# Last stage of a fused attention and state-space backward kernel: another order of its loads, shared tiles, and repeated columns copied on the chip

## The chip, the cores and the metric

The kernel runs on one core of a Trainium2 chip. The metric is the device time of one execution in microseconds (us). Lower is better. Every time below is from the timed runs, or from one execution taken by the hardware profiler, whose page and trace are queried in many views. PE is TensorE, PEld its weight loads, DVE VectorE, ACT ScalarE, POOL GpSimd, SP SyncE, which issues most of the transfers here.

## What is computed

The reference is the backward pass (and the output) of a gated mix of two branches over a sequence of 2048 tokens and 576 channels, in bf16:

```
g = sigmoid((x * gate_w).sum(-1))
a = attention(x, wqkv) @ wo                 # 32 heads of 18 channels
b = ssm_convolution(u = constant, A, B, C, log_dt) + skip   # 128 complex states per channel
out = g * a + (1 - g) * b
grads of x, wqkv, wo, A, B, C, log_dt, Dskip, gate_w for a given grad_out
```

In the last stage these are left: the output itself, the gradient of x (out_1), of wqkv (out_2), of wo (out_3), of the six parameter matrices A, B, C (out_4 to out_9, each 576 x 128), and some vectors.

## The kernel before

The kernel has a first stage (projections), an attention stage, a state-space stage in 18 blocks of 32 channels (for i in range(NBLK)), and the last stage, from about line 1563 to line 1778, which alone is changed. Tiles of 128 partitions are used throughout. The work of the last stage, in the order of the code:

**Loads on SP (lines 1589 to 1610).** zz takes four rows of precomputed state powers (par_d), dt_b the time steps, Wri two more rows of par_d, prm5 the six parameter matrices, wo_sb the matrix wo, wqkvT the transposed wqkv in ten transposing transfers, O_tok the attention output of all 16 token tiles (columns 0 to 575 by one transfer, line 1607, and columns 576 to 639, a repetition of the last 64, by another, line 1608), go_all the whole gradient, gate_b a broadcast row. Each transfer waits on SP until the place that it fills is no longer read, and SP issues strictly in its order. Where a tile lies, and so whose readers it must wait for, is decided by the pools (pf, pfx, pfw, pbwork, pbot): a pool opened after others were closed takes their addresses.

**dwq (line 922).** dwq(u, cs) computes one column quarter u of the gradient of wqkv for chunks cs of 128 rows: 16 matmuls of 427 or 448 columns each into one PSUM tile (tag "one", two buffers), an ACT copy to dwq_bf (three buffers), and a store on POOL's queue. Quarter 2 is loaded into a tile of its own late in the last block; quarters 1 and 3 lie in tiles of tag E1n. dwq_last does the last 64 rows of quarters 2 and 3 together.

**Parameter chain on DVE (lines 1634 to 1681).** Some 60 elementwise operations of 128 x 576 turn the sums SS and CK of the state-space stage into the six parameter gradients. It begins with eight operations on the rows Zr, Zi, then the two negations of Wri (lines 1634 and 1635), then four groups of four with zr, zi, then products with Wr, Wi and the parameter matrices. Each finished matrix is multiplied by dt into a padded tile opad (six of them), turned on PE in five 128 x 128 transposes (emit_dn, line 1619: PSUM tile opt, two buffers), copied by ACT (obo, two buffers) and stored by POOL. PE's order of this part is written by hand: dwq(1), dwq(2), the first two opt, two chunks of dwq(3), two opt, the rest of dwq(3), dwq_last, two opt, and two small matmuls fr.

**Token loop (lines 1690 to 1737).** For each of 16 token tiles t: every fourth t the transposed attention output OT4 of four tiles is made by a transposing transfer out of O_tok; every second t the rows y_b and dxr_b of two tiles are loaded from yd_d (which the last block of the state-space stage still writes: the store of line 807); dqT, the transposed gradient of qkv, is made by two transposing transfers. PE computes ps_a = OT4 @ wo (10 matmuls) and ps_dx = J @ dxr + dqT @ wqkvT (30 matmuls), both in the PSUM tag ps2b with two buffers. DVE forms dif = ps_a - y, o0b (the output rows), an accumulation with go_all, and o1b (the x gradient, from ps_dx); POOL stores o0b and o1b. Buffers: y_b and dxr_b four each, dqT three, o0b three, o1b two, dif two, OT4 two.

**Tail.** A row of 64 small matmuls for gate_w (pgw), then the wo gradient (ps_dwo, 160 matmuls over all token tiles) and its stores.

A hand-written order (manual_schedule) holds for PE and SP in the first part; elsewhere the order is found by a scheduler when the program is built. Every transfer of SP uses one of eight completion semaphores in turn, so it also waits for the transfer eight places ahead of it to have landed.

Of the kernel before, what the change touches and what calls it, by code (L numbers as in the profile page):

```python
# [9 lines left out]
A = mybir.AluOpType  # L10
ACT = mybir.ActivationFunctionType
BF = mybir.dt.bfloat16
F32 = mybir.dt.float32
# [4 lines left out]
P = 128  # L18


def build(tc, aps, dbg_aps=None, stages=("s1", "attn", "post", "s4", "final")):
    nc = tc.nc
# [39 lines left out]
    with ExitStack() as gctx:  # L62
# [66 lines left out]
        with ExitStack() as ctx:  # L129
# [183 lines left out]
            def tt(o, a, b, op):  # L313
                V.tensor_tensor(o, a, b, op=op)
# [1247 lines left out]
        if "final" in stages and "s4" in stages:  # L1562
# [7 lines left out]
            with ExitStack() as ctx:  # L1570
# [9 lines left out]
                tt(ggo, g_t, omg_t, A.mult)  # L1580

                with ExitStack() as actx:
                    actx.enter_context(tc.manual_schedule(engines={mybir.EngineType.PE, mybir.EngineType.SP}))
                    pf = actx.enter_context(tc.tile_pool(name="pf", reuse_waits="tile", bufs=1))
                    Q["nob"] = 3
                    pfw = Q["pbw"] = actx.enter_context(tc.tile_pool(name="pfw", reuse_waits="tile", bufs=2))

                    zz = pf.tile([P, 4, D], F32, name="zz")
                    for q, r_ in enumerate((0, 2, 8)):
                        n_ = 2 if r_ == 8 else 1  # L1590
                        nc.sync.dma_start(zz[:, q:q + n_, :], par_d[:, r_:r_ + n_, :])
                    dt_b = pf.tile([P, D], F32, name="dt_b5")
                    nc.sync.dma_start(dt_b, dt_d)
                    prm5 = pf.tile([P, 6, D], BF, name="prm5")
                    pfx = actx.enter_context(tc.tile_pool(name="pfx", reuse_waits="tile", bufs=1))
                    Wri = pfx.tile([P, 2, D], F32, name="Wri_f")
                    nc.sync.dma_start(Wri, par_d[:, 6:8, :])
                    Wr_n, Wi_n = Wri[:, 0, :], Wri[:, 1, :]
                    nc.sync.dma_start(prm5, prm_d)
                    nc.sync.dma_start(wo_sb[:, 0:nf, :], wo[0:nf * P, :].rearrange("(c p) n -> p c n", p=P))  # L1600
                    for x in range(2):
                        nc.sync.dma_start(wo_sb[x * HB:(x + 1) * HB, nf, :], wo[nf * P:D, :])
                    dwq(1, range(nf), "one", 2)
                    for c, (d0, dsz) in enumerate(dch):
                        for k0_, k1_, f0 in ((0, FZ // P, 0), (FZ // P, FC, FZ - ZP)):
                            nc.sync.dma_start_transpose(out=wqkvT[:, k0_:k1_, d0:d0 + dsz], in_=wqkv[d0:d0 + dsz, f0:f0 + (k1_ - k0_) * P])
                    nc.sync.dma_start(O_tok[:, :, 0:D], O_d)
                    nc.sync.dma_start(O_tok[:, :, D:DPAD], O_d[:, :, D - HB:D])
                    nc.sync.dma_start(go_all, go_v)
                    nc.sync.dma_start(gate_b, gate_w.rearrange("(o d) -> o d", o=1).to_broadcast([P, D]))  # L1610
                    dwq(2, range(nf), "one", 2)

                    opad = []
                    for q in range(6):
                        o_q = pf.tile([P, DPAD], BF, name=f"opad{q}")
                        nc.gpsimd.memset(o_q[:, D:DPAD], 0.0)
                        opad.append(o_q)

                    def emit_dn(out_ap, a, b, idx):
                        o_q = opad[idx]  # L1620
# [10 lines left out]
                    Ar_n, Ai_n, Br_n, Bi_n, Cr_n, Ci_n = [prm5[:, r_, :] for r_ in range(6)]  # L1631
                    ta = pf.tile([P, D], F32, name="fta")
                    o_t = pf.tile([P, D], F32, name="o_t")
                    nc.vector.tensor_scalar(Wr_n, Wr_n, -1.0, None, op0=A.mult)
                    nc.vector.tensor_scalar(Wi_n, Wi_n, -1.0, None, op0=A.mult)
                    Zr_, Zi_, zr_, zi_ = [zz[:, q, :] for q in range(4)]
# [7 lines left out]
                    for (Sr_, Si_, u, kc) in ((S0r, S0i, 0, 0), (S1r, S1i, 2, 1)):  # L1644
# [3 lines left out]
                        nc.vector.scalar_tensor_tensor(Si_, ta, -1.0, CK[:, 1, kc, :], op0=A.mult, op1=A.subtract)  # L1648
                    glr, gli, Tdt = zr_, zi_, s_[0]
                    tt(glr, Wr_n, S1r, A.mult); tt(ta, Wi_n, S1i, A.mult); tt(glr, glr, ta, A.add)  # L1650
# [7 lines left out]
                    dwq(3, (0, 1), "one", 2)  # L1658
# [4 lines left out]
                    dwq(3, range(2, nf), "one", 2)  # L1663
# [4 lines left out]
                    Tb = pf.tile([P, D], BF, name="Tb")  # L1668
                    nc.vector.tensor_copy(Tb, Tdt)
                    row = pf.tile([1, D], F32, name="dlrow")  # L1670
# [4 lines left out]
                    rowb = pf.tile([1, D], BF, name="dlrowb")  # L1675
                    nc.vector.tensor_copy(rowb, row)
                    nc.gpsimd.dma_start(aps_out["out_10"].rearrange("(o d) -> o d", o=1), rowb)
                    rowb2 = pf.tile([1, D], BF, name="ddsrowb")
# [3 lines left out]
                work = ctx.enter_context(tc.tile_pool(name="pbwork", reuse_waits="tile", bufs=2))  # L1682
                wot = ctx.enter_context(tc.tile_pool(name="pbot", reuse_waits="tile", bufs=2))
                sgo = pb.tile([P, NT], F32, name="sgo")
                dsg = pb.tile([P, NT], F32, name="dsg")
                dsgb = pb.tile([P, NT], BF, name="dsgb")
                OT4 = None
                YB = 2
                for t in range(NT):
                    if t % TB == 0:  # L1690
                        OT4 = wot.tile([P, TB, DC, P], BF, tag="OT4", name="OT4")
                        nc.sync.dma_start_transpose(out=OT4.rearrange("p t c q -> p (t c) q"),
                                                    in_=O_tok[:, t:t + TB, :].rearrange("p t d -> p (t d)"))
                    if t % YB == 0:
                        y_b = work.tile([P, YB, D], BF, tag="y_b", bufs=4, name="y_b")
# [124 lines left out]
```

## Times and profile before

| | us |
|---|---|
| timed runs: median (lowest, highest of 3) | 2711.42 (2704.62, 2716.91) |
| profiled execution | 2694.2 |
| its span | 2692.3 |
| its mean granted TensorE clock | 0.97 |
| misc matmuls of the last block, start | 2523.0 |
| first ps_a of the token loop, start | 2579.4 |
| last ps_dx of the token loop, end | 2669.1 |
| ps_dwo, start and length | 2670.2, 17.8 |

How to read the views. The busy table gives, for stretches of time, the busy us of each engine with the number of instructions, then the granted TensorE clock as a share of full speed, the mean busy share of the 16 DMA engines (which can exceed 1 where packets overlap), and GB/s. The view of waits says which engine waited for whom, with the total, the number of waits and the longest. The timeline lists instructions with start and length; for a transfer on SP the length is the time that the queue took to issue it, not the time until it landed. The chain of waits goes back from the last instruction, at each step to what released it.

On the page DVE is busy 85%, PE 89% and ACT 87% of the span; in the last 150 us ACT and POOL are mostly idle and the DMA engines are busy 0.9 or more nearly until the token loop ends.

### The profile page before, as it was taken

To read this page: it belongs to the slowest core of one execution; us is meant where nothing else is said; L and a number is where in the kernel's file an instruction comes from. 1 tells how busy PE (TensorE), PEld (TensorE's weight loads), DVE (VectorE), ACT (ScalarE), POOL (GpSimd) and SP (SyncE) were. 2 spreads that over 40 slices of the span, in tenths; PEclk is the share of its full clock that TensorE was granted. 3 is DMA by queue.
4 is the path that set the end of the run, shared out by engine and by line. 5 is a ranking of instruction groups with operands and counts; after the bars stand their busy time and mean duration, and the time that the engine had idled before them with its cause. 6 is when DMAs were issued, how large, how long until landed. Compare 5 with 4: busy or idle time off the path is not lost.

```text
span 2692.3 us, 70041 instructions
## 1 busy us (share of the span) xinstructions
PE 2404.9 (89%) x27411; PEld 1138.0 (42%) x27411; DVE 2300.6 (85%) x4142; ACT 2343.5 (87%) x2726; POOL 1786.8 (66%) x2829
## 2 busy tenths in 40 slices
PE   8898888998989899998989989898987799999889
PEld 4433333333333333333333333333322689998556
DVE  5649899999989999898999999899986599999854
ACT  5489999999999999999999999999984599898211
POOL 0278888888888888888878888887811144445321
PEclk9889999999999999999999999999996799999989
DMA  7637789879978978987998898789769788887895
GB/s 231 187 98 161 153 167 173 168 156 184 171 150 168 185 155 163 181 168 153 167 177 155 160 179 161 154 168 177 147 131 212 184 246 259 252 255 235 233 265 124
DMA packets 1158165, 485.71 MB, mean 180 GB/s; under 512 B 1072581, under 2 KB 1112118, under 8 KB 1155530
## 3 DMA queue, kind: packets, MB, share of 16 engines
q1 hardware_dynamic: 1112074, 341.62, 63.7%
q0 software_dynamic: 43744, 134.11, 18.3%
q10 hardware_dynamic: 2016, 5.51, 0.7%
q8 instruction: 214, 3.51, 0.6%
q14 instruction: 117, 0.96, 0.1%
HBM read 145.94 MB, written 93.21 MB: 89 GB/s over the span
## 4 chain that ended last, share of the span: by engine, by line
ACT 39%; PE 25%; DVE 24%; issue 6%; DMA 3%; POOL 2%; SPq 1%; ACTq 0%; DVEq 0%; POOLq 0%
ACT eb L1384 23%; ACT PT L1379 15%; DVE ds L1389 7%; PE ps_P L30 7%; DVE tz L730 3%; PE accV L30 2%; PE ps_dx L30 2%; PE turn_p L1092 2%; PE ps_proj L30 2%; DVE tz L733 2%; DVE HG L735 1%; DVE wa L749 1%; DVE wb L749 1%; DVE pq L810 1%; PE accK L30 1%
## 5 line engine op out<-in xcount | busy, mean ns | idle before, releaser
L1389 DVE TENSOR_TENSOR ds<-ps_P,PT 128x512 bf16<-128x512 f32 x2048 | 1312.2, 683 | 122.9 <-PE ps_P L30 84.8
L1384 ACT ACTIVATE eb<-ps_P 128x1024 bf16<-128x1024 f32 x1024 | 1101.2, 1076 | 30.6 <-PE ps_P L30 30.5
L1379 ACT ACTIVATE PT<-ps_P 128x1024 bf16<-128x1024 f32 x1024 | 1106.3, 1081 | 19.6 <-PE ps_P L30 18.4
L30 PE MATMUL ps_P<-dOaT,VaT_g 32*128 32x512 bf16 x2048 | 580.6, 387 | 31.3 <-DVE ds L1389 15.8
L503 POOL TENSOR_TENSOR et<-eG,eT 128x448 f32<-128x448 f32 x576 | 542.2, 961 | 10.7
L30 PE MATMUL ps_P<-QaT_g,KaT_g 32*128 32x512 bf16 x2048 | 400.8, 384 | 137.8 <-ACT PT L1379 124.4
L30 PE MATMUL ps_P<-KaT_g,QaT_g 32*128 32x512 bf16 x2048 | 404.9, 388 | 2.1 <-ACT eb L1384 1.6
L30 PEld LDWEIGHTS <-KaT_g 32*128 32x128 bf16 x2048 | 147.9, 91 | 467.6 <-issue 451.3
L503 POOL TENSOR_TENSOR Eo<-et,et 128x448 bf16<-128x448 f32 x288 | 326.8, 1135 | 20.7
L30 PEld LDWEIGHTS <-QaT_g 32*128 32x128 bf16 x2048 | 116.0, 91 | 285.0 <-issue 262.2
L30 PE MATMUL accV<-eb,dOa 128*32 128x512 bf16 x2048 | 185.1, 394 | 27.2 <-ACT eb L1384 27.0
L30 PE MATMUL accO<-PT,Vtok_g 128*32 128x512 bf16 x2048 | 206.6, 393 | 0.1
L30 PE MATMUL accK<-dsT,Qtok_g 128*32 128x256 bf16 x4096 | 161.5, 278 | 12.3 <-DMA dsT<-ds 10.5
L30 PE MATMUL accQ<-ds,Ktok_g 128*32 128x512 bf16 x2048 | 161.6, 394 | 2.1 <-DVE dvacc L1146 2.0
L30 PEld LDWEIGHTS <-Vtok_g 128*32 128x32 bf16 x2048 | 52.7, 93 | 222.2 <-issue 222.2
L1097 DVE COPY dsT<-turn_p 128x1024 bf16<-128x1024 bf16 (+1 forms) x216 | 139.2, 644 | 2.1 <-PE turn_p L1092 2.1
L1092 PE MATMUL turn_p<-ident_bf,ds 128*128 128x128 bf16 x1664 | 132.9, 222 | 1.9 <-DVE gb L1164 0.8
L669 ACT COPY E1e<-etp 128x1024 bf16<-128x1024 bf16 x132 | 125.3, 1062 | 2.6 <-PE etp L668 2.6
L503 POOL TENSOR_TENSOR et<-eT 128x32 f32<-128x32 f32 (+3 forms) x288 | 115.8, 422 | 11.4
L30 PEld LDWEIGHTS <-Qtok_g 128*32 128x32 bf16 x4096 | 87.3, 96 | 76.7 <-issue 63.3
L1092 PEld LDWEIGHTS <-ds 128*128 128x128 bf16 x1664 | 96.4, 98 | 49.4 <-issue 49.3
L1044 POOL TENSOR_TENSOR dOa<-dO_b,rl 128x288 bf16<-128x288 bf16 x32 | 21.5, 673 | 143.0 <-DVE rl L1039 142.9
(289 smaller groups left out, 3733.6 us busy)
## 6 DMA issues: line engine op xcount, KB each, us to landing
E_d<-Eo POOLq DMA_DIRECT2D x144, 256.0 KB, 3.3
E1n<-E_d POOLq DMA_DIRECT2D x30, 1024.0 KB, 6.5
T0w<-Kp_d SPq DMA_DIRECT2D x18, 1024.0 KB
xs<-xb_d POOLq DMA_DIRECT2D x28, 512.0 KB, 9.7
dsT<-ds SPq DMA_TRANSPOSE x512
dqkv_d<-dtk POOLq DMA_DIRECT2D x96, 72.0 KB, 4.2
Md_d<-mst SPq DMA_DIRECT2D x18, 288.0 KB
skw<-Md_d SPq DMA_DIRECT2D x72, 64.0 KB
```

The source lines that it names most:

```text
L30: return nc.tensor.matmul(out, lhsT=lhsT, rhs=rhs, start=start, stop=stop, **kw)
L503: nc.gpsimd.tensor_tensor(out, a, b, op=op)
L669: copy(E_[:, 4 * q:4 * q + 4], pt_)
L730: nc.vector.tensor_tensor(tz[x], HG[:, :, k - 1].unsqueeze(1).to_broadcast([P, 2, 2, n, CB]), ZZ.unsqueeze(3).to_broadcast([P, 2, 2, n, CB ...
L733: nc.vector.tensor_tensor(tz[x][:, 0], tz[x][:, 0], UVk[:, :, :, k, :], op=A.add)
L735: nc.vector.tensor_tensor(HG[:, :, k], tz[x][:, 0], tz[x][:, 1, ::-1], op=A.add)
L749: nc.vector.tensor_tensor(B_[nm], B_["HG"].rearrange("p r k s c -> p (r k s) c"), par_of(b)[:, r_, :].unsqueeze(1).to_broadcast([P, 4 * NS ...
L1092: nc.tensor.transpose(pt_[:, x, qb, :], t_[:, qb * P:(qb + 1) * P], ident_bf)
L1097: (nc.scalar.copy if NTOT <= now[0] < NTOT + OFF else nc.vector.tensor_copy)(o_(), pt_[:, x:x + n])
L1379: nc.scalar.activation(U["PT"][i, j // 2], ps, ACT.Exp)
L1384: nc.scalar.activation(e, ps, ACT.Exp)
L1389: nc.vector.tensor_tensor(U["ds"][i][:, j, :], ps, U["PT"][i, j // 2][:, j % 2, :], op=A.mult)
```

## The change

All in the last stage:

- The loads are issued in another order: zA (rows 0 and 2 of par_d in one transfer) and zB (rows 8 and 9), wo_sb, dt_b, prm5 in two halves, O_tok, Wri, wqkvT, then the first OT4, the first y and the first two dqT, then go_all, gate_b and the second OT4.
- The tiles of the parameter chain stay allocated to the end (pf and pfw in the outer context), and the token loop takes its tiles from the same places by tag: y_b and dxr_b share one tile out of Wri, zA, zB; dqT uses the two prm places and two E1n tiles; dif uses fta and o_t; o0b and o1b use opad and Tb; the wo gradient's store tile uses row, rowb, rowb2. opad has four places for six matrices.
- The second load of O_tok (repeated columns) is replaced by an ACT copy on the chip.
- The negations of Wri come after the eight plus sixteen operations that don't need them.
- dwq(3) is computed right after dwq(1); two chunks of dwq(2) come before the first opt, two after it.
- PE's order is also written by hand in the token loop, and the built order weaves the last two opt and the fr matmuls into token 0's ps_dx; the first two ps_a matmuls stand before the fourth opt. dwq_last comes between them and the rest.

```diff
                 with ExitStack() as actx:
...
-                    pf = actx.enter_context(tc.tile_pool(name="pf", reuse_waits="tile", bufs=1))
+                    pf = ctx.enter_context(tc.tile_pool(name="pf", reuse_waits="tile", bufs=1))
                     Q["nob"] = 3
-                    pfw = Q["pbw"] = actx.enter_context(tc.tile_pool(name="pfw", reuse_waits="tile", bufs=2))
-                    zz = pf.tile([P, 4, D], F32, name="zz")
-                    for q, r_ in enumerate((0, 2, 8)):
-                        n_ = 2 if r_ == 8 else 1
-                        nc.sync.dma_start(zz[:, q:q + n_, :], par_d[:, r_:r_ + n_, :])
-                    dt_b = pf.tile([P, D], F32, name="dt_b5")
-                    nc.sync.dma_start(dt_b, dt_d)
...
-                    nc.sync.dma_start(Wri, par_d[:, 6:8, :])
-                    Wr_n, Wi_n = Wri[:, 0, :], Wri[:, 1, :]
-                    nc.sync.dma_start(prm5, prm_d)
+                    zA = tile_("zA", [P, 2, D], F32, "zA")
+                    zB = tile_("zB", [P, 2, D], F32, "zB")
...
+                    NOP = 4
...
+                    nc.sync.dma_start(zA, par_d[:, 0:4:2, :])
+                    nc.sync.dma_start(zB, par_d[:, 8:10, :])
                     nc.sync.dma_start(wo_sb[:, 0:nf, :], wo[0:nf * P, :].rearrange("(c p) n -> p c n", p=P))
                     for x in range(2):
                         nc.sync.dma_start(wo_sb[x * HB:(x + 1) * HB, nf, :], wo[nf * P:D, :])
+                    nc.sync.dma_start(dt_b, dt_d)
+                    for q in range(2):
+                        nc.sync.dma_start(prm5[q], prm_d[:, 3 * q:3 * q + 3, :])
+                    nc.sync.dma_start(O_tok[:, :, 0:D], O_d)
+                    nc.sync.dma_start(Wri, par_d[:, 6:8, :])
+                    Wr_n, Wi_n = Wri[:, 0, :], Wri[:, 1, :]
                     dwq(1, range(nf), "one", 2)
+                    nc.scalar.copy(O_tok[:, :, D:DPAD], O_tok[:, :, D - HB:D])
                     for c, (d0, dsz) in enumerate(dch):
                         for k0_, k1_, f0 in ((0, FZ // P, 0), (FZ // P, FC, FZ - ZP)):
                             nc.sync.dma_start_transpose(out=wqkvT[:, k0_:k1_, d0:d0 + dsz], in_=wqkv[d0:d0 + dsz, f0:f0 + (k1_ - k0_) * P])
-                    nc.sync.dma_start(O_tok[:, :, 0:D], O_d)
-                    nc.sync.dma_start(O_tok[:, :, D:DPAD], O_d[:, :, D - HB:D])
...
+                    def load_y(t, y_):
+                        nc.sync.dma_start(y_[:, 0], yd_d[:, 0, t:t + YB, :])
+                        nc.sync.dma_start(y_[:, 1], yd_d[:, 1, NT - YB - t:NT - t, :])
+                        return y_
...
+                    dwq(3, range(nf), "one", 2)
+                    wot = ctx.enter_context(tc.tile_pool(name="pbot", reuse_waits="tile", bufs=2))
+                    load_ot(0)
+                    y0 = load_y(0, en_tile("y_b")[:, 0:2 * YB * D].rearrange("p (x t d) -> p x t d", x=2, d=D))
+                    dq_a = en_tile("dqT")
+                    dqT0 = [load_dqT(t, dq_a[:, t * FPAD:(t + 1) * FPAD].rearrange("p (c q) -> p c q", q=P)) for t in range(2)]
                     nc.sync.dma_start(go_all, go_v)
                     nc.sync.dma_start(gate_b, gate_w.rearrange("(o d) -> o d", o=1).to_broadcast([P, D]))
-                    dwq(2, range(nf), "one", 2)
+                    load_ot(TB)
...
-                    nc.vector.tensor_scalar(Wr_n, Wr_n, -1.0, None, op0=A.mult)
-                    nc.vector.tensor_scalar(Wi_n, Wi_n, -1.0, None, op0=A.mult)
...
+                    nc.vector.tensor_scalar(Wr_n, Wr_n, -1.0, None, op0=A.mult)
+                    nc.vector.tensor_scalar(Wi_n, Wi_n, -1.0, None, op0=A.mult)
                     glr, gli, Tdt = zr_, zi_, s_[0]
+                    dwq(2, (0, 1), "one", 2)
...
-                    dwq(3, (0, 1), "one", 2)
+                    dwq(2, range(2, nf), "one", 2)
...
-                    dwq(3, range(2, nf), "one", 2)
                     dwq_last(2, 3, "one", 2)
...
+                ctx.enter_context(tc.manual_schedule(engines={mybir.EngineType.PE}))
                 for t in range(NT):
...
                     if t % YB == 0:
-                        y_b = work.tile([P, YB, D], BF, tag="y_b", bufs=4, name="y_b")
-                        nc.sync.dma_start(y_b, yd_d[:, 0, t:t + YB, :])
-                        dxr_b = work.tile([P, YB, D], BF, tag="dxr_b", bufs=4, name="dxr_b")
-                        nc.sync.dma_start(dxr_b, yd_d[:, 1, NT - YB - t:NT - t, :])
+                        yx = y0 if t == 0 else load_y(t, tile_(("Wri", "zA", "zB")[t // YB % 3], [P, 2, YB, D], BF, "y_b"))
+                        y_b, dxr_b = yx[:, 0], yx[:, 1]
...
-                    dqT = work.tile([P, FC, P], BF, tag="dqT", bufs=3, name="dqT")
+                    if t < 2:
+                        dqT = dqT0[t]
+                    elif t % 4 >= 2:
+                        dqT = load_dqT(t, tile_(f"prm{t % 4 - 2}", [P, FC, P], BF, "dqT"))
+                    else:
+                        dqT = load_dqT(t, en_tile("dqT")[:, 0:FPAD].rearrange("p (c q) -> p c q", q=P))
```

## The prediction

> **What bounds the kernel now.** I read the page first: the change touches only what follows the last state-space block, so of the span of 2692.3 us only the end counts. The busy table in stretches of 5 us then shows which engine stands there (columns after the length: busy us and instruction count of PE, PE weight loads, DVE, ACT and POOL, then granted TensorE clock, DMA share, GB/s).
>
> ```profile
> 2545.00:2550.00 5.00, 4.79 (x27) 2.37 (x25) 4.90 (x8) 0.65 (x2) 0.97 (x2) 1.00 1.06 253
> 2550.00:2555.00 5.00, 0.00 (x0) 0.00 (x0) 4.96 (x9) 0.38 (x1) 0.54 (x1) 0.95 0.86 157
> 2555.00:2560.00 5.00, 3.70 (x17) 2.02 (x18) 5.00 (x8) 1.38 (x2) 2.56 (x4) 0.50 0.96 283
> ...
> 2575.00:2580.00 5.00, 1.86 (x18) 0.80 (x14) 0.45 (x1) 2.32 (x4) 3.56 (x6) 0.84 1.11 229
> 2580.00:2585.00 5.00, 2.28 (x10) 0.99 (x10) 0.89 (x2) 0.00 (x0) 0.65 (x2) 0.50 1.05 247
> 2585.00:2590.00 5.00, 3.92 (x16) 2.20 (x16) 2.50 (x5) 0.77 (x1) 0.59 (x1) 0.50 0.96 203
> ...
> 2600.00:2605.00 5.00, 5.00 (x41) 3.49 (x40) 3.24 (x7) 0.78 (x1) 1.08 (x2) 1.00 0.83 297
> ```
>
> PE is full before 2549.6 and from 2594 to the end (2688), and has two holes between; after each its clock is 0.50. The waits of PE in 2545 to 2600 name what ended them (times, longest):
>
> ```profile
> PE opt L1624 <- DVE opad L1568: 6.5, 2, 5.2
> PE ps_dx L30 <- DMA dxr_b<-yd_d: 3.6, 1, 3.6
> PE ps_a L30 <- DMA OT<-O_tok: 3.1, 1, 3.1
> PE ps_dx L30 <- DMA dqT<-dqkv_d: 0.2, 1, 0.2
> ```
>
> Hole one is the DVE parameter chain, hole two the first token's loads. The SP queue in order of time (start, length) says why both are late:
>
> ```profile
> 2517.38 0.32 SPq L1593 DMA_DIRECT2D dt_b<-dt_d  x1
> 2533.58 0.32 SPq L1597 DMA_DIRECT2D Wri_f<-par_d  x1
> 2533.95 0.43 SPq L1599 DMA_DIRECT2D prm<-prm_d  x1
> ...
> 2536.29 17.42 SPq L1606 DMA_TRANSPOSE wqkvT<-in_A_wqkv_dram  x10
> 2553.82 0.59 SPq L1607 DMA_DIRECT2D O_tok<-O_d  x1
> 2554.46 3.47 SPq L1608 DMA_DIRECT2D O_tok<-O_d  x1
> 2558.04 6.91 SPq L1609 DMA_DIRECT2D go_all<-in_grad_out_dram  x1
> 2564.99 2.63 SPq L1610 DMA_DIRECT2D gate_b<-in_gate_w_dram  x1
> 2567.79 12.47 SPq L1692 DMA_TRANSPOSE OT<-O_tok  x2
> ```
>
> Wri takes the place of a tile read by the last yd_d store (issued 2524.46, landed 2533.5), and everything behind it in SP's order waits with it; DVE loses 4.1 us for Wri itself. From 2533.5 the transfers run nearly without a pause, yet OT lands only at 2579.4. Once PE is in the token loop nothing on it waits; the chain of waits shows one token (start, length):
>
> ```profile
> 2598.09 1.31 PE ps_a L30 x10
> 2599.40 3.77 PE ps_dx L30 x30
> ```
>
> **What the holes cost.** From 2549.6 to the end of token 0's ps_dx (2593.25) are 43.65 us. The work in them, at the full-clock rows: four 448-wide dwq groups at 3.05 = 12.2, dwq_last 3.2, six opt at 0.28 = 1.7, fr 0.25, ps_a 1.31, ps_dx 3.77, three matmuls of the next ps_a 0.4: 22.8. Lost: 20.9, of which 13.5 is idle (5.22, 1.29, 3.14, 3.62, 0.19) and 7.4 is slow clock. Here **a rule and the trace differ**: the Trainium skill, TensorE: Matmul & The Clock Gate, section Part 1: The HAM clock gate, says the clock halves after an idle window of about 3.4 us and is restored after about 3.4 us of work, that is 1.7 us per cold stretch, 3.4 for two; by the rule the holes cost 16.9, by the rows 20.9. The rows are of this very stretch, so I take 20.9.
>
> **Part by part.** *Order of loads.* In the built order each load waits only for the last reader of its own place. Set against the trace's times: zA, zB 2504.9 as before; wo_sb once the last yp<-RX,T0w is done (2510.3); dt and both prm at 2517.4; O_tok after the last yp<-Rw,E1n (2523.2); Wri after half of the misc matmuls (about 2525). None waits for yd_d any more; the first OT does. DVE then starts at 2527.7 as now and first needs Wri after 8 + 16 + later operations, at 2546. O_tok (2.36 MB) shares the engines with the dq load still running and with the yd_d store: together about 4.2 MB from 2525 at the 322 GB/s of 2558 to 2565, done about 2538; Wri (0.59 MB) about 2540, landed by 2542. So the 4.1 us of DVE go, with 4 us to spare.
>
> *dwq order.* PE gets all of dwq(3) and half of dwq(2) before the first opt: from 2526.33 4 x 2.92 + 4 x 3.05 + 2 x 2.92 = 29.7, to 2556.0. The first opad, now done at 2555.0, comes at 2551.7 and the second at 2553.8. Hole one is closed; its cover is those six groups. dq(3) landed before 2515, dq(2) by 2540.
>
> *Transposes and first token.* The ten wqkvT transposes take SP 1.25 to 1.4 us each; the seventh waits for O_tok's landing (2540), the eighth for Wri, so they end about 2547. *Repeated columns:* a 256 KB load in 2048 packets of 128 B (3.47 us of issue) becomes one ACT copy of 128x1024 elements, 1.06 us by the nearest row (L669, 1062 ns). ACT has idle time, but its queue puts the copy behind the third dwq(3) evacuation (2547.8), so it ends at 2548.9 and OT is issued then. Queued behind that wait on SP: the second-token loads, go_all, gate. OT lands 2555, y 2556, dqT for two tokens 2561 (SP needs 6.4 for the four). PE reaches the first ps_a at 2562.5 and ps_dx at 2567.4: hole two is closed with 6 us to spare. go_all is now last: issued 2560, drained about 2570, needed by DVE's accumulation at 2573.
>
> *Reused tiles.* y has 3 places and one extra instead of 4 and 4, dqT 4 instead of 3, dif, o0b and o1b as many as before. dqT of token t waits for ps_dx of t-4: three tokens' lead, 15 us, against 4.8 us from issue to use at 2582.4 to 2587.2. Cost none in steady state; without that cover each token would pay up to 4.8. New waits: ps_dx(1) waits for dif(1), which stands on DVE behind dlrow, o0b and the accumulation: 1.6 us. The second OT is queued behind go_all on the ring, then y, then dqT(2): in the present trace dqT(0) was usable 12.2 us after go_all had drained (2575 to 2587.2, with two OTs, not one), so about 8 here, 2578 against the need at 2580. Bounds for the unshown: dif wait 0.5 to 2.5 us, late dqT(2) 0 to 4 us; nearest row says 0.
>
> *Contention.* The skill's DMA: Bandwidth & Descriptors, section Issuing engines are not separate DMA queues, speaks against the change: a load moved ahead on SP takes engine time from POOL's stores. Rows: with DMA share 0.98 to 1.44 at 2535 to 2550 the dwq stores still landed in 4.2 us (median), and three buffers at 2.92 us tolerate about 7.7. The same page (Queues, rings and completion order) has each engine take turns between the queues; by the rule as a plain halving of POOL's rate, yd_d lands at 2539 instead of 2533.5 and the first dwq store at 2540, when ACT wants its buffer at 2538.1 and PE needs that evacuation at 2541.1: no loss, 0 to 2 in the range.
>
> **Sum.** PE after: 2556.0 + opt 0.6 + two dwq 5.8 + opt and ps_a 0.8 + dwq_last 3.2 + ps_a 1.05 + ps_dx with opt and fr 4.6 = 2572.0; ps_a(1) 1.3, wait 1.6, ps_dx(1) 3.8: 2578.7. Before, ps_dx(1) ended at 2598.0. That is 19.3 us; everything after it (fourteen tokens, pgw, ps_dwo, the last store, 94.3 us) is the same PE work. I take 1.8 off for dqT(2) and stores: **17.5 us**. The profiled execution took 2694.2 us (span 2692.3 and 1.9 around it) and would take 2676.7. The three timed runs lie higher, 2704.62 to 2716.91; the profiled one is 17 below their median, so I subtract from the median: 2711.4 - 17.5 = **2694 us**.
>
> **Rivals.** A measurement of this kernel can tell about 0.5% (13.6 us) from no change.
> 1. *The forecast:* both holes closed, 15 to 20 us, 2691 to 2697. For: the work to fill them is in the built order. Chance 0.60.
> 2. *Supply takes over:* total bytes hardly fall and the engines are full from 2533 on; PE meets late dqT or go_all in tokens 0 to 5 and falls cold again. Two stops of 3 us and half clock (7.4 / 2 each) cost 10: gain 5 to 13, about 2702. For: DMA share about 1.0 until 2645. Against: within the loop SP itself waited for PE about 20 us, so supply is faster than demand. Chance 0.24.
> 3. *The wait is only renamed:* OT, y and go_all end as late as now because the saturated engines do not start earlier in effect; gain 0 to 5, 2709. For: 2.36 MB + 2 MB + 2.36 MB must still pass. Against: share 0.31 and 0.48 at 2515 to 2525 and 0.40 at 2530 to 2535 leaves 9 us of engine time unused. Chance 0.08.
> 4. *Slower:* POOL's stores behind O_tok and the transposes. Place: ACT's dwq evacuations, three buffers. Below a landing time of 7.7 us it costs nothing; above, each group of the ten pays a third of the excess, so it outweighs 19.3 us at a landing of 13.5 us or more: at 15 us it costs 24, net 5 slower, 2716. For: dq took 10.0 and yd_d 9.0 us to land. Against: the 4.2 above. Chance 0.08.
>
> **Numbers.** Range: down to 2684 (no stop, 20.9, and the 6 us by which the medians of such runs may differ), up to 2709 (rival 3); the ends leave out about 0.2. Faster by over 0.5%: rival 1 and little of 2: 0.62; within: 0.29; slower: 0.09 (rival 4 and noise on 3).
>
> **What would show it.** PE without a hole over 2 us between 2526 and the end, granted clock 1.00 in every 5 us stretch; the Wri wait of DVE gone; O_tok issued about 2523, OT about 2549; first ps_a about 2562; token period still 5.08. The forecast is wrong if PE's waits name DMA dqT, OT or go_all (rival 2 or 3), or ACT's dwq_bf waits for stores (rival 4).

## The result, and the profile after

Over six runs each the median fell from 2710.15 us to 2693.68 us, ratio 0.993 (95% interval 0.9906 to 0.9953). The profiled execution of the changed kernel took 2687.22 us, its span 2685.5. A second set of runs gave 0.9954 (0.9936 to 0.9971), so the two intervals overlap between 0.9936 and 0.9953, which is a gain of 13 to 17 us.

Spans of single executions can't be set against each other here: the first dwq(1) matmul, ahead of which PE's work is the same in all kernels, starts between 2526.3 and 2551.0 us in the 14 executions shown below. All stage times are therefore counted from that matmul (0) to the end of the span. **Before: 166.0 us** (2526.33 to 2692.3). **After: 153.6** (2531.86 to 2685.5), in a second execution 154.3. The stage itself gained 11.7 to 12.3 us; the prediction had 19.3 for the sum and 17.5 after its allowance.

The waits of PE from 2526 us to the end (in total, times, longest) show where the difference is: both holes of before are gone, and one new stop has come.

```profile
PE ps_dx L30 <- DVE dif L1762: 5.7, 1, 5.7
```

The busy table in 5-us stretches puts it at 2579 to 2585, with the clock at half behind it. It was 1.00 in every stretch from 2525 to there.

```profile
2575.00:2580.00 5.00, 4.08 (x34) 2.56 (x33) 1.90 (x4) 1.32 (x2) 2.21 (x4) 1.00 1.08 369
2580.00:2585.00 5.00, 0.22 (x2) 0.13 (x2) 1.66 (x5) 0.78 (x1) 1.50 (x3) 0.80 1.20 264
2585.00:2590.00 5.00, 5.00 (x23) 3.12 (x22) 2.22 (x5) 0.78 (x1) 1.13 (x2) 0.52 1.15 272
2590.00:2595.00 5.00, 5.00 (x41) 3.49 (x40) 3.29 (x6) 0.13 (x1) 1.08 (x2) 1.00 1.24 244
```

The wait names DVE's dif, but DVE had itself been waiting. The chain of waits (start, length) follows it back:

```profile
2565.10 1.48 SPq L1661
...
2570.23 1.94 SPq L1661
2572.17 0.04 issue
2572.22 10.98 DMA go_all<-in_grad_out_dram
...
2583.29 0.77 DVE dif L1765 x2
2584.06 0.68 DVE dif L1762
2584.74 0.04 issue
2584.78 6.28 PE ps_dx L30 x30
2591.07 1.31 PE ps_a L30 x10
2592.38 3.77 PE ps_dx L30 x30
```

Read from below: a normal ps_dx takes 3.77 us, the one after the stop 6.28 (2.5 us of slow clock). It waited for dif(1), which stands on DVE behind token 0's accumulation (L1765), which waited for go_all, which was issued at 2572.2 and landed at 2583.2. DVE's own waits agree: "DVE dif L1765 <- DMA go_all<-in_grad_out_dram: 4.5, 1, 4.5". Why go_all was so late, SP's queue shows (start, length of issue):

```profile
2527.05 0.58 SPq L1639 DMA_DIRECT2D O_tok<-O_d  x1
2530.43 8.48 SPq L1640 DMA_DIRECT2D Wri_f<-par_d  x1
2539.13 20.09 SPq L1646 DMA_TRANSPOSE wqkvT<-in_A_wqkv_dram  x10
2559.60 3.52 SPq L1651 DMA_TRANSPOSE OT<-O_tok  x1
```

O_tok is issued early, as forecast, but the issue of Wri behind it takes 8.48 us instead of 0.32, and the ten transposes 20.09. They end 27.4 us after the first dwq matmul, just where they ended before the change (2553.71, also 27.4). The first OT is nevertheless issued at 27.7 instead of 41.5, because O_tok, its columns, go_all and gate_b no longer stand between the transposes and it. The first ps_a, which waited for this load before, starts 36.2 us after the first dwq matmul instead of 53.1.

The packets of all queues show when the transposing loads, which come in packets under 512 B, really pass. The first line is for 2531.9 to 2544.9 us, the second for 2544.9 to 2558.9:

```profile
DMA packets 2354, 4.34 MB, mean 333 GB/s; under 512 B 111, under 2 KB 1773, under 8 KB 2353
DMA packets 8300, 2.78 MB, mean 199 GB/s; under 512 B 8088, under 2 KB 8093, under 8 KB 8298
```

In the first 13 us next to none of them move; then they take 14 us.

### The profile page after: what moved, and what is told of

It is laid out like the page before. It is cut to its first block, busy times and chain, and to the rows that moved or that the text cites. A ratio compares the mean times of both kernels' runs of the same rounds, so it can differ in the third digit from the quotient of the medians.

```text
span 2685.5 us, 70035 instructions
## 1 busy us (share of the span) xinstructions
PE 2404.0 (90%) x27411; PEld 1141.2 (42%) x27411; DVE 2299.9 (86%) x4142; ACT 2345.2 (87%) x2727; POOL 1787.2 (67%) x2827
## 4 chain that ended last, share of the span: by engine, by line
ACT 40%; PE 25%; DVE 24%; issue 6%; DMA 3%; SPq 1%; ACTq 0%; POOL 0%; DVEq 0%; POOLq 0%
ACT eb L1384 24%; ACT PT L1379 15%; DVE ds L1389 8%; PE ps_P L30 7%; DVE tz L730 3%; PE accV L30 2%; PE ps_dx L30 2%; PE turn_p L1092 2%; DVE tz L733 2%; DVE HG L735 1%; DVE pq L810 1%; DVE wa L749 1%; PE accK L30 1%; DVE wb L749 1%; DVE dvacc L1146 1%
## 5 line engine op out<-in xcount | busy, mean ns | idle before, releaser
L503 POOL TENSOR_TENSOR Eo<-et,et 128x448 bf16<-128x448 f32 x288 | 326.9, 1135 | 20.7
L30 PE MATMUL accV<-eb,dOa 128*32 128x512 bf16 x2048 | 184.9, 394 | 27.4 <-ACT eb L1384 27.3
```

The costliest lines, as they stand in the source:

```text
L30: return nc.tensor.matmul(out, lhsT=lhsT, rhs=rhs, start=start, stop=stop, **kw)
L503: nc.gpsimd.tensor_tensor(out, a, b, op=op)
```

## The experiments

Every run names its stage length, from the first dwq(1) matmul to the end, and the stops of PE in it. Each length is that of one execution. Between the two executions of the changed kernel it differed by 0.7 us, so only clearly more than that is read. The ratios are to the kernel before, with their 95% intervals; they move with what happens ahead of the stage and are the coarser measure.

| run | stage, us | stops of PE, us | ratio |
|---|---|---|---|
| before | 166.0 | opt 6.5, OT 3.1, dxr 3.6 | 1 |
| after | 153.6 | ps_dx(1) for go 5.7 | 0.993 (0.9906 to 0.9953) |
| k_after_again | 154.3 | ps_dx(1) for go 6.8 | 0.9954 (0.9936 to 0.9971) |
| a_go_split | 156.1 | OT 2.3, dif 4.6, dqT 1.3 | 0.9958 (0.9942 to 0.9974) |
| b_go_front | 154.4 | OT 2.2, dqT 1.6, y 1.5, dif 0.9 | 0.9952 (0.9935 to 0.997) |
| c_cols_dma | 154.5 | ps_dx(1) for go 6.3 | 0.9958 (0.9939 to 0.9978) |
| d_dwq_order | 156.5 | opad 2.9, o1b 2.7, dqT 3.0 | 0.9971 (0.9953 to 0.9988) |
| e_split_both | 154.4 | fr 3.8, dqT 1.2, dif 0.9 | 0.9949 (0.9929 to 0.9968) |
| f_plain_w | 148.7 | dqT 1.8, dif 1.1 | one run |
| g_hold | 158.4 | dif 6.0, OT 3.1, dqT 1.1 | 0.9953 (0.9927 to 0.9979) |
| h_o_late | 158.5 | dif 4.5, OT 4.0 | one run |
| i_split_paced | 154.0 | dqT 3.2, dif 1.9 | 0.9955 (0.9935 to 0.9975) |
| j_before_dwq | 165.9 | OT 10.2, dxr 3.9, opad 1.3, dqT 1.1 | 1.0003 (0.9985 to 1.0021) |
| l_split_three | 155.5 | dqT 2.7, y 2.6, dif 2.0 | 0.9941 (0.9921 to 0.9961) |

**First question: is the new stop only go's place in the order?** The theory says yes (order, S); its rival says that the bytes decide (B).

a_go_split: go of two tokens and gate_b ahead of the first OT.

```diff
+                    nc.sync.dma_start(go_all[:, 0:2, :], go_v[:, 0:2, :])
+                    nc.sync.dma_start(gate_b, gate_w.rearrange("(o d) -> o d", o=1).to_broadcast([P, D]))
                     load_ot(0)
...
-                    nc.sync.dma_start(go_all, go_v)
-                    nc.sync.dma_start(gate_b, gate_w.rearrange("(o d) -> o d", o=1).to_broadcast([P, D]))
+                    nc.sync.dma_start(go_all[:, 2:NT, :], go_v[:, 2:NT, :])
```

> Edit: go for the first two tokens (0.29 MB) and gate_b are loaded ahead of the first OT, the other fourteen tokens of go where all of it was. The same bytes, another order. Theory S (the 5.7 us stop of ps_dx(1) is the place of go in the order): the accumulation of token 0 no longer waits, ps_dx(1) starts within 1.6 us of the end of ps_a(1), no cold stretch; OT and dqT come some 1.5 us later (0.44 MB at about 300 GB/s), of which 0 to 2 us reach PE. From the first dwq matmul to the end 146 to 149 us, against 153.6 of the changed kernel and 166.0 of the kernel before. Theory B (the bytes decide: the engines are full, whatever comes last is late): the stop reappears at OT, dqT or the rest of go with 4 us or more, 151 to 155 us.

Measured: 156.1. Token 0 no longer waits for go, but the first OT is 2.3 us late, and ps_dx(2) stops 3.5 us for dif(2), which itself waited 3.1 us for y of token 2, queued behind the rest of go. The stop has moved by one token; theory S falls. Theory B has the mechanism, though the stage is 1.1 us above its bracket. The waits of PE:

```profile
PE ps_dx L30 <- DVE dif L1763: 4.6, 2, 3.5
PE ps_a L30 <- DMA OT<-O_tok: 2.3, 1, 2.3
PE ps_dx L30 <- DMA dqT<-dqkv_d: 1.3, 1, 1.3
```

b_go_front: all of go ahead of the transposes.

```diff
                     Wr_n, Wi_n = Wri[:, 0, :], Wri[:, 1, :]
                     dwq(1, range(nf), "one", 2)
...
+                    nc.sync.dma_start(go_all, go_v)
+                    nc.sync.dma_start(gate_b, gate_w.rearrange("(o d) -> o d", o=1).to_broadcast([P, D]))
                     for c, (d0, dsz) in enumerate(dch):
```

> Edit: all of go (2.36 MB) and gate_b are loaded right after Wri, ahead of the ten wqkvT transposes. Theory S (order): the DVE wait for go goes, but OT and dqT come about 7.5 us later (2.36 MB at 310 GB/s), so PE stops at the first ps_a or ps_dx(0) for 4 to 7 us and runs cold behind it; since everything must have landed before ps_dx(1) in both orders, the stage is about as long as now, 152 to 156 us against 153.6. If instead the transposes are limited by their own issue and not by bytes, go passes beside them and the stage is 145 to 149 us.

Measured: 154.4, within its first bracket. The wait for go is gone, and OT, y and dqT are late instead; the stage is the same. The transposes did not pass beside go: they ended 35.0 us after the first dwq matmul instead of 27.4.

**Second question: what did each part of the change give?** One part is undone at a time.

c_cols_dma: the repeated columns by a transfer again.

```diff
                     nc.sync.dma_start(O_tok[:, :, 0:D], O_d)
+                    nc.sync.dma_start(O_tok[:, :, D:DPAD], O_d[:, :, D - HB:D])
...
-                    nc.scalar.copy(O_tok[:, :, D:DPAD], O_tok[:, :, D - HB:D])
```

> Edit: the repeated columns of O_tok by a DMA again (right after O_tok), the copy on ACT gone. Theory S: 2048 packets of 128 B more in a full queue, everything behind it on SP 2 to 3.5 us later (3.5 us was its issue in the kernel before), go with it; the stop of ps_dx(1) grows from 5.7 to 8 or 9 us and the stage from 153.6 to 156 or 157. If the copy was worth nothing: 153.6 within 0.5.

Measured: 154.5, and the stop 6.3. Against the two executions of the changed kernel (153.6 and 154.3, stops 5.7 and 6.8) no difference can be told. The 3.5 us expected were the issue time in an order in which the transposes came first. Here the issue of the columns took 10.47 us, and yet the transposes ended at 28.7 us after the first dwq matmul, against 27.4 and 28.4 without it.

d_dwq_order: dwq as in the kernel before.

```diff
-                    dwq(3, range(nf), "one", 2)
+                    dwq(2, range(nf), "one", 2)
...
-                    dwq(2, (0, 1), "one", 2)
...
-                    dwq(2, range(2, nf), "one", 2)
+                    dwq(3, (0, 1), "one", 2)
...
+                    dwq(3, range(2, nf), "one", 2)
                     dwq_last(2, 3, "one", 2)
```

> Edit: the dwq groups in the order of the kernel before (dwq(2) ahead of the chain, dwq(3) between the opt), the loads as changed. PE has 8 groups instead of 10 ahead of the first opt, so it would wait 0.7 us for the first opad and 1.3 us for the second. Theory S: go is the limit at a fixed time, so these 2 us come off the 5.7 us stop and the stage stays at 153.6 within 1 us; the waits of PE show opad about 2 us and ps_dx(1) 3.5 to 4 us. Rival (the order of dwq was itself worth what the prediction gave it in hole one): 2 to 5 us longer, 155.6 to 158.6.

Measured: 156.5, that is 2.2 to 2.9 us longer: the rival's bracket, but not the rival's way. As theory S said, the 2.9 us of waiting for opad came off the go stop. ps_dx(1) waited 2.7 us instead of 5.7, for o1b of token 0, which stood behind the same accumulation:

```profile
DVE dif L1765 <- DMA go_all<-in_grad_out_dram: 3.9, 1, 3.9
```

ps_dx(1) even ended earlier, 57.3 us after the first dwq matmul instead of 59.2. What theory S left out came behind it: dqT of token 2 was 3.0 us late, and PE ran at half clock after that.

g_hold: SP stands ahead of O_tok until yd_d has landed, as it did for Wri before.

```diff
+                    nc.sync.dma_start(rowb[:, 0:HB], yd_d[0:1, 0, 0, D - HB:D])
                     nc.sync.dma_start(O_tok[:, :, 0:D], O_d)
```

> Edit: ahead of O_tok a 128-byte load that reads yd_d, so that SP stands there until the last yd_d store has landed, as it stood for Wri in the kernel before (7.3 us after the first dwq matmul); all else as changed. Theory Q (the gain is the head start of the queue, 12 us): O_tok is issued at about +7 instead of -4.8, OT, y, dqT and go come 9 to 12 us later, first ps_a at 45 to 49 us, stage 161 to 166 us, that is most of the 12.3 us gain gone. Rival (the gain lies in the order of dwq, the copy on ACT and the reused tiles): 154 to 159 us.

Measured: 158.4, the rival's bracket, so most of the gain is not the head start: O_tok was issued 13.1 us later (+8.3 instead of -4.8), but the transposes ended only 5.1 us later (32.5 instead of 27.4), and the stage lost 4.1 to 4.8. Three fifths of the queue's head start are spent waiting in it: with SP held, the engines move mostly what POOL had asked for (1.76 of 2.60 MB in the 13 us from the first dwq matmul), and then Wri's issue takes 3.35 us instead of 8.48.

h_o_late: O_tok and its columns behind the transposes.

```diff
-                    nc.sync.dma_start(O_tok[:, :, 0:D], O_d)
                     nc.sync.dma_start(Wri, par_d[:, 6:8, :])
...
-                    nc.scalar.copy(O_tok[:, :, D:DPAD], O_tok[:, :, D - HB:D])
...
                             nc.sync.dma_start_transpose(out=wqkvT[:, k0_:k1_, d0:d0 + dsz], in_=wqkv[d0:d0 + dsz, f0:f0 + (k1_ - k0_) * P])
+                    nc.sync.dma_start(O_tok[:, :, 0:D], O_d)
+                    nc.scalar.copy(O_tok[:, :, D:DPAD], O_tok[:, :, D - HB:D])
```

> Edit: O_tok and the copy of its columns behind the ten transposes, as in the kernel before; Wri and the transposes are then first. Theory Q (what counts is when the queue starts and what it holds, not the order within it): OT is issued at about the same time as now or up to 4 us later (it has to wait for O_tok's landing and for the copy in ACT's queue), stage 153 to 158 us against 153.6. Rival (the order of loads, O_tok early, is itself the gain): OT 8 us or more later, stage 160 us or more.

Measured: 158.5, just outside the first bracket (153 to 158), 4.2 to 4.9 us longer than the change; OT was issued 5.7 us later (33.5 instead of 27.7), because it has to wait for O_tok's landing. The place of O_tok in the order is worth that much.

j_before_dwq: the kernel before with only the dwq order of the change.

```diff
-                    dwq(2, range(nf), "one", 2)
+                    dwq(3, range(nf), "one", 2)
...
+                    dwq(2, (0, 1), "one", 2)
...
-                    dwq(3, (0, 1), "one", 2)
+                    dwq(2, range(2, nf), "one", 2)
...
-                    dwq(3, range(2, nf), "one", 2)
                     dwq_last(2, 3, "one", 2)
```

> Edit: the kernel before with the dwq order alone changed (dwq(3) and half of dwq(2) ahead of the first opt), all loads as before. By the prediction's step, hole one is closed by these groups. Theory Q: the first OT lands at a time that the queue sets, 53 us after the first dwq matmul, so closing hole one only makes hole two longer; what is saved is one cold stretch, 2 to 4 us: stage 162 to 164 us against 166.0. If hole one is worth its own idle and clock time by itself: 6.5 idle and 3 to 4 cold, stage 156 to 158 us.

Measured: 165.9 against 166.0, ratio 1.0003: nothing, less even than the one cold stretch that theory Q allowed. The waits of PE:

```profile
PE ps_a L30 <- DMA OT<-O_tok: 10.2, 1, 10.2
PE ps_dx L30 <- DMA dxr_b<-yd_d: 3.9, 1, 3.9
PE opt L1624 <- DVE opad L1568: 1.3, 2, 0.7
```

Hole one is closed (6.5 to 1.3), and the wait for OT has grown from 3.1 to 10.2. ps_dx(0) starts at 59.3 us after the first dwq matmul, against 59.6: idle time ahead of a transfer with a fixed landing only moves. PE stood 16.5 us instead of 13.5, and by subtraction the slow clock cost about as much less. With the loads as changed the stage was 2.2 to 2.9 us shorter with this order (d_dwq_order).

Undone one at a time, then, the hold on SP costs 4.1 to 4.8 us, O_tok behind the transposes 4.2 to 4.9, the dwq order 2.2 to 2.9, and the copy nothing that can be told. Since a stop closed in one place comes back in another, these are not shares that add up to the gain. No run undid the reuse of the tiles or the later place of the two negations.

**Third question: is it the bytes or the transposing loads?** Theory Q is now that SP's queue is never empty, and that everything waits for what is ahead of it.

f_plain_w: plain loads of as many bytes in the transposes' place; wqkvT then holds other values, and the transposition is left out.

```diff
+                    wflat = wqkvT.rearrange("p c d -> p (c d)")
+                    o_w = 0
...
-                            nc.sync.dma_start_transpose(out=wqkvT[:, k0_:k1_, d0:d0 + dsz], in_=wqkv[d0:d0 + dsz, f0:f0 + (k1_ - k0_) * P])
+                            n_w = (k1_ - k0_) * dsz
+                            nc.sync.dma_start(wflat[:, o_w:o_w + n_w], wqkv[0:P, 0:n_w])
+                            o_w += n_w
```

> Edit: the ten transposing loads of wqkvT replaced by ten plain loads of as many bytes (wqkvT then does not hold the transposed weight; this leaves out the transposition). Theory Q: the ten transposes hold the queue for 20.1 us for 2.0 MB, plain loads would need 6 to 8; all behind them 12 us earlier, no stop of PE over 2 us, stage 145 to 147 us against 153.6. If bytes alone count and not their form: the queue is as long as now, stage 152 to 155 us.

Measured: 148.7, two thirds of the expected gain, in one execution. SP was through the ten loads in 10.19 us instead of 20.09, and the clock was 1.00 throughout. But go_all was issued only 6.9 us earlier, since SP then stood for the ACT copy of the columns, which the transposes had covered until then:

```profile
SPq L1655 <- ACT O_tok L1643: 4.8, 1, 4.8
```

The traffic in the two stretches, after first (2544 to 2559.2 us), then this run (2549.6 to 2559.8 us):

```profile
DMA packets 8495, 3.22 MB, mean 212 GB/s; under 512 B 8164, under 2 KB 8200, under 8 KB 8493
```

```profile
DMA packets 2335, 3.74 MB, mean 366 GB/s; under 512 B 210, under 2 KB 1684, under 8 KB 2334
```

The second stretch still begins with the rest of O_tok and Wri; from 2557.7 to 2561.5 us, when both are through, it is 379 GB/s. The transposing loads come in packets under 512 B, and with them the engines, busy either way, move 212 GB/s. So the form of these loads, at the same bytes, is part of what sets how late go is. Of 148.7 us another 2.8 are idle (1.1, 0.8, 0.9), so PE's own work in the stage is about 145.8 us; the change's 153.6 less 5.7 idle and 2.5 slow clock gives 145.4.

e_split_both, i_split_paced, l_split_three: O_tok and go in pieces, so that 2.9 to 3.5 MB pass behind the first two tokens. The core of the first, and what the other two change in it:

```diff
-                    nc.sync.dma_start(O_tok[:, :, 0:D], O_d)
+                    nc.sync.dma_start(O_tok[:, 0:TB, 0:D], O_d[:, 0:TB, :])
...
                     load_ot(0)
+                    nc.sync.dma_start(go_all[:, 0:TB, :], go_v[:, 0:TB, :])
...
-                    nc.sync.dma_start(go_all, go_v)
-                    nc.sync.dma_start(gate_b, gate_w.rearrange("(o d) -> o d", o=1).to_broadcast([P, D]))
-                    load_ot(TB)
+                    nc.sync.dma_start(O_tok[:, TB:NT, 0:D], O_d[:, TB:NT, :])
+                    nc.scalar.copy(O_tok[:, TB:NT, D:DPAD], O_tok[:, TB:NT, D - HB:D])
+                    nc.sync.dma_start(go_all[:, TB:NT, :], go_v[:, TB:NT, :])
```

```diff
# i_split_paced, in the token loop
+                    if t == 3:
+                        nc.scalar.copy(O_tok[:, TB:NT, D:DPAD], O_tok[:, TB:NT, D - HB:D])
+                        load_ot(TB)
+                    if t == 5:
+                        nc.sync.dma_start(go_all[:, 2 * TB:NT, :], go_v[:, 2 * TB:NT, :])
# l_split_three, in the token loop
+                    if t == 5:
+                        nc.sync.dma_start(O_tok[:, 2 * TB:NT, 0:D], O_d[:, 2 * TB:NT, :])
+                        nc.sync.dma_start(O_tok[:, 2 * TB:NT, D:DPAD], O_d[:, 2 * TB:NT, D - HB:D])
+                        nc.sync.dma_start(go_all[:, 2 * TB:NT, :], go_v[:, 2 * TB:NT, :])
```

> Edit: only the first four tokens of O_tok (0.59 of 2.36 MB) ahead of Wri and the transposes, with their columns copied on ACT; go for four tokens and gate_b behind the first OT; then y and dqT(0,1), and only then the other twelve tokens of O_tok and go; the second OT behind dqT(2). All bytes stay, 3.5 MB of them move behind the first two tokens. Theory Q (supply: SP's queue works through its bytes without a pause, and the first tokens have to wait for all that is ahead of them): 3.5 MB at 310 GB/s are 11 us, the end of the transposes comes at about 18 to 21 us after the first dwq matmul instead of 27.4, OT, go and dqT(1) before PE asks; no stop of PE over 2 us, stage 145 to 147 us against 153.6. If order is all the same because the later tokens meet the moved bytes: a stop at OT(4), dqT(2) or go of 4 to 8 us, 151 to 155 us.

Measured: 154.4, in the second bracket but for another reason. There was no stop for go or OT; but PE's fr waited 3.8 us for an ACT evacuation, and the waits of ACT say what stood ahead of it:

```profile
ACT O_tok L1676 <- DMA O_tok<-O_d: 8.3, 1, 8.3
```

The second copy of columns, which this edit itself put into ACT's queue, waited there for its transfer, with the evacuation behind it. The run therefore tells little of the theory.

> Edit: as in the split of both O_tok and go, with its own new wait taken away: the columns of the later twelve tokens of O_tok are copied on ACT behind the dwq evacuations (after token 3's loads in the program), go comes in two halves (eight tokens behind the first OT, eight after token 5's loads), and the loads of the token loop are issued in the program's order. Theory Q (the first tokens wait for what is ahead of them in the queue; 1.8 MB of O_tok and 1.2 MB of go can pass behind them): no stop of PE over 2 us and no cold stretch, stage 145.5 to 148 us against 153.6 and 154.4 of the first split. If the moved bytes only move the stop: a stop of 3 to 6 us at dqT(2), OT(4) or go, stage 150 to 155 us.

Measured: 154.0, the second bracket. The copy is off the path, but with go for eight tokens ahead of it dqT(0) was 3.2 us late.

> Edit: O_tok and go in pieces as the tokens need them: tokens 0 to 3 as in the first split (O_tok ahead of Wri, go behind the first OT), 4 to 7 behind dqT(1), 8 to 15 after token 5's loads; columns of tokens 4 to 15 by DMA, so that nothing on ACT waits for O_tok; the loop's loads in the program's order. Theory Q: 0.29 MB less ahead of y and dqT than in the paced split (go for four tokens, not eight, which cost it a 3.2 us stop at dqT(0)), 2.4 MB not in the queue before dqT(2): no stop over 2 us, stage 146.5 to 149.5 us, as the plain-load run with its 148.7. If stops remain whatever the order, because the transposing loads alone fill the queue up to token 1: 151 to 155 us.

Measured: 155.5, 0.5 above the last bracket. Up to token 5 there was no stop over 2.03 us; the second piece of O_tok and go (2.5 MB, issued around token 4) then held up y and dqT of token 6:

```profile
2599.21 0.58 SPq L1755 DMA_DIRECT2D O_tok<-O_d  x1
2599.84 0.58 SPq L1756 DMA_DIRECT2D O_tok<-O_d  x1
2600.46 2.48 SPq L1757 DMA_DIRECT2D go_all<-in_grad_out_dram  x1
2602.99 3.15 SPq L1655 DMA_DIRECT2D y_b<-yd_d  x1
2606.19 0.44 SPq L1656 DMA_DIRECT2D y_b<-yd_d  x1
2606.72 10.10 SPq L1661 DMA_TRANSPOSE dqT<-dqkv_d  x4
```

Four dqT transposes take 10.10 us there, against 6 to 9 earlier in the same run. So theory Q held for the queue and not for its use. Seven arrangements of nearly the same bytes (after with its repeat, a, b, c, e, i, l) lie between 153.6 and 156.1, most with their stop in another place; d_dwq_order, g_hold and h_o_late are longer (156.5 to 158.5), and only f_plain_w, with larger packets, is clearly shorter. No run moved clearly fewer bytes.

k_after_again: the changed kernel unedited.

> The changed kernel once more, unedited, beside the others on one chip. The stage is repeatable: 153.6 us within 0.5, the stop of ps_dx(1) 5.7 us within 0.5. If these 12.3 us are all that the change gives, the ratio to the kernel before is 0.9955 (12.3 of 2710); if the change also shortens something ahead of the stage, it is 0.993 as first measured.

Measured: 154.3 (0.2 outside its bracket), the stop 6.8, ratio 0.9954: the figure that the stage's own gain would give. That the change shortens something ahead of the stage is not supported.

No version that computes everything beat the changed kernel; the intervals of a, b, e, i and l all overlap with its own.

## Why the prediction was right, and where it was wrong

The predicted median, 2694 us, was met (2693.68), and the likeliest case, two closed holes, came about. But the agreement is in part luck. The sum behind it was too large by half (19.3 against 12.6 us), and the scatter of the medians made up for it: 12 us off the median 2711.4 would have been 2699, and the second set of runs gave 13.7 us between medians. By the prediction's own signs, no hole over 2 us and a clock of 1.00 in every stretch, the mechanism came out only in part.

- **What bounds, and the 20.9 us lost.** Right. Floor of the stage after 145.4, before 166.0 - 20.9 = 145.1: the same PE work, twice. So is the tail: predicted 94.3 us after ps_dx(1), measured 94.4 (2591.07 to 2685.5), and the token period stayed 5.08.
- **Hole one.** Right, to a tenth: the first opt was to come 29.7 us after the first dwq matmul and came at 29.6; PE has no wait there and DVE none for Wri. What the prediction didn't say, and j_before_dwq shows, is that this step has no value by itself.
- **Hole two.** First ps_a predicted at 36.2, measured 36.24; first ps_dx 41.1, measured 41.07. Right. The ACT copy took 1.05 us for the estimated 1.06 and ended at 22.5 as forecast (22.6). But OT was not "issued then", SP being busy with the transposes until 27.4; the first ps_a did not wait all the same.
- **The step that failed: "The ten wqkvT transposes take SP 1.25 to 1.4 us each; the seventh waits for O_tok's landing (2540), the eighth for Wri, so they end about 2547."** That is 20.7 us after the first dwq matmul; they ended at 27.4. The step let six of the ten overlap with O_tok and priced only their issue. O_tok and Wri did land about when forecast (their last packets are at 13.3 and 15.1 us, forecast 13.7 and 15.7). But SP stood 8.48 us in the issue of Wri, so the first transpose was issued only at 7.3, and the small packets began to pass when O_tok's had, at 13.1, and took 14 us. The single issue was right (1.28 us in the middle); the time that the packets need to pass was not in the sum. The trace of before had the ten at 17.42, printed in the prediction itself, and it took the least and the middle one of these ten instead. Why SP stood so long in Wri's issue stays open. It is not simply the 2.36 MB of O_tok ahead: in b_go_front the same load behind the same O_tok took 0.35 us, and gate_b, two transfers on, 15.24; in h_o_late, without O_tok ahead, the first transpose took 7.16.
- **What followed from it.** go_all was to be issued at 33.7 and drained at 43.7, three us ahead of the need; it was issued at 40.4 and landed at 51.3. The term "wait 1.6" for dif(1) became 5.7, and the cold stretch that it brought, 2.5, was not in the sum at all. These two, 4.1 + 2.5 = 6.6, are the shortfall of the sum, 19.3 against 12.6 (measured at the end of ps_dx(1): 71.8 before, 59.2 after). The allowance of 1.8, meant for dqT(2) and stores, stood for something that didn't happen.
- **Rivals.** Rival 2 had the mechanism: PE "meets late dqT or go_all in tokens 0 to 5 and falls cold again", gain 5 to 13. It came once, not twice, beside the closed holes, so the truth lay between rival 1 and rival 2, and its main argument against ("supply is faster than demand" in the loop) did not cover the first tokens. Rival 3 fell. Rival 4 fell: ACT never waited for a dwq store in the changed kernel; these landed in 3.3 and 5.6 us (medians of the 112 and 107 KB stores). The slowest took 7.9, a little over the 7.7 from which the prediction expected a cost, and still nothing waited for it.
- **Contention.** "No loss" holds for the stores. What POOL's transfers take from SP's loads was in the sum (4.2 MB until O_tok is through), and O_tok came about when forecast, although from 2532 to 2538 us POOL's queue moved 1.47 of the 1.93 MB and SP's only 0.44.
- **The clock.** The prediction took the rows (7.4 us for the two stretches) over the Trainium skill's rule, TensorE: Matmul & The Clock Gate, Part 1: The HAM clock gate (1.7 each). The new stop cost 2.5, between them.

## What to carry to other kernels

When a whole stage's loads are issued one behind another, work out when the last byte that a consumer needs has passed the queue, not when its transfer is issued; closing an idle hole ahead of that moment gained nothing here (165.9 against 166.0). Cost a transfer by the row of the same transfer under load (here 17.4 us for ten in the trace of before), not by one free issue. And when several orders of the same bytes give the same time with the stop in another place, look at the form of the transfers (here larger packets, 148.7 against 153.6) before trying another order.

## What was not expected of the hardware

- Transposing loads take about twice as long to pass as plain ones of the same size here: 14 us at 199 GB/s, nearly all in packets under 512 B, against 379 GB/s where the plain loads pass. SP's own stretches, 20.09 and 10.19 us for 2.0 MB, are not prices of issuing, since SP waits within them: in f_plain_w 5.8 us for the landing of O_tok, Wri and one of the loads. The Trainium skill, Advanced Engine Details and Errata, section X-Bar Transpose (TRN2), has transposing transfers as fast as plain ones, 350 to 400 GB/s; in this kernel the runs decide otherwise.
- Where SP's queue begins at the same time, the end of the transposes' issue depends on the bytes ahead of them in SP's order almost as a line: 20.6 us with O_tok behind them (h_o_late), 22.7 to 23.0 with 0.59 MB ahead (e, i, l), 27.4 and 28.4 with 2.36 MB (after, repeat), 35.0 with 4.87 MB (b). That is 14.4 us for 4.87 MB, 3.0 us per MB, or about 340 GB/s. g_hold, whose queue begins 13.1 us later, lies off it (32.5 with 2.36 MB).
- How long PE must stand before the clock halves is no fixed number: an idle time of 3.1 us (g_hold) left it at 1.00, while one of 3.2 and a later one of 1.9 (i_split_paced) did not. What is regular is how long it stays at half: 3.4 us (d, twice in i), 6.8 (after, repeat, a, b, c, e, g, l, twice in h, once each in before and j), 10.2 (j) or 13.7 us (before), all multiples of 3.4. This agrees with the free-running window of about 3.4 us that the Trainium skill's clock page (same section as above) describes. The 6.8 us of the changed kernel, of which 5.1 came after work had resumed, cost 2.5.

What stays open: whether pieces of O_tok and go spread evenly over the tokens, or a wqkvT transposed on PE, would bring the stage to its 145.5 us, and whether DVE could take dif of token 1 ahead of token 0's accumulation, which alone needed go_all when ps_dx(1) stopped. None of these was tried.
